# Block-sparse attention and a gated MLP on one core: leftover output products in other PSUM banks, two stores on another queue

## The chip, the cores and the metric

The kernel runs on one core of one Trainium2 chip. The metric is the device time of one execution in microseconds (us). Each engine of the core has its own instruction stream: PE (TensorE) multiplies matrices into PSUM, PEld is its weight load, ACT (ScalarE) and DVE (VectorE) read PSUM and write SBUF, POOL (GpSimd) does casts, SP (SyncE) mostly issues DMAs. Both SP and ACT can issue a DMA, and each instruction waits for semaphores of the work that it depends on.

## The reference

Attention under a block mask (window, first and last block, sampled blocks), and then a gated MLP with a spatial product per batch. B is 4, H 8, S 768, D 64, d_model 512, d_ff 1024. Cut to what matters:

```python
scores = np.where(mask, scale * q @ k.T, -1e9)
attn = exp(scores - max) ; attn = attn / (attn.sum(-1) + 1e-9)
x = (attn @ v).transpose(0, 2, 1, 3).reshape(B, S, H * D)
h = np.maximum(x @ w_in, 0.0)
u, v = h[..., :512], h[..., 512:]
v_n = (v - mean(v)) / sqrt(var(v) + 1e-6)
v_s = einsum('ts,bsd->btd', w_spatial, v_n) + b_spatial[None, :, None]
out = (u * v_s) @ w_out
```

## The kernel before, in words

The work is written out by hand, slot by slot (lines 880 to 898). In a slot PE makes the scores of one key chunk (`qk_full`, line 481) into a PSUM tile with tag "sc" (two buffers of two banks each), ACT takes the exponential, and seven slots later `av_full` (line 533) multiplies with the values into a tile with tag "av" (two buffers). DVE normalizes the result (`normalize`, lines 500 to 504: a reciprocal and a product). The MLP of batch b is a queue of single matmuls, `Moe` (line 627), dealt into the slots of batch b + 1; its PSUM tiles have the tags "moeA" and "moeB", one buffer each, in turn.

The MLP of a batch has six row chunks `tcc` of 128 tokens and four kinds of products, each a group of matmuls into one PSUM tile (`product`, line 608):

- v and u products (four matmuls), drained with a Relu by ACT or DVE.
- s products (six matmuls, the spatial product). DVE drains them into `un` (line 687), and SP then issues a DMA transpose of `un` into `gt` (line 697), two chunks at a time, or one at a time for the last two chunks of the last batch.
- o products (four matmuls with `gt` as weights), here called o0 to o5. ACT or DVE copies the tile to `osb` (six buffers, lines 714 and 715), and a DMA stores it (line 716). For batch 2, ACT copies o0, o2 and o4, and DVE o1, o3 and o5. For the last batch the even ones go to ACT, the odd to DVE, and o5 is made in two halves of 256 columns: the first is copied by DVE and stored by SP, the second copied and stored by ACT.

When the slots end, `last_x` (line 825) empties what is left of the queue, the **leftover**: three o products of batch 2, o3, o4 and o5. By then `ended` is set. It then begins the MLP of batch 3: the first matmuls of v0 and v1, six transposes of the last attention output into a bank of the "moe" pair, two DVE copies of that (`xt`), and the rest. From there no attention is left.

The PSUM tile of a product comes from `moe_ps` (line 598). While attention runs it is the "moe" pair. For the leftover and for all of batch 3, the deque `tail_tags` turns through "moe", "av" and "sc", so that all six buffers are used in turn. So in the kernel before, o3 has a tile of the "moe" pair (the one that o1 had), o4 one of "av", o5 one of "sc".

The stores of batch 3 in the kernel before: o0 by ACT; o1 to o4 and the first half of o5 by SP; the second half of o5 by ACT. SP issues the four transposes of batch 3 ahead of them, here T01, T23, T4 and T5 by their chunks; T45 is the last transpose of batch 2. DMAs of SP are the queue q1 of the profile, those of ACT q10.

Of the kernel before, what the change touches and what calls it, by code (L numbers as in the profile page):

```python
# [10 lines left out]
FP32 = mybir.dt.float32  # L11
# [15 lines left out]
def kernel(  # L27
# [16 lines left out]
    nc = tc.nc  # L44
# [27 lines left out]
    psum = ctx.enter_context(tc.tile_pool(name="psum", bufs=1, space=bass.MemoryType.PSUM))  # L72
# [219 lines left out]
    def moe_tag():  # L292
        moe_tags.rotate(1)
        if moe_tags[0] in held:
            moe_tags.rotate(1)
        return moe_tags[0]
# [301 lines left out]
    def moe_ps(last):  # L598
        if not (last or ended):
            return psum.tile([128, 512], FP32, tag=moe_tag(), bufs=1, name="ps_moe")  # L600
        tail_tags.rotate(1)
        if tail_tags[0] == "sc":
            return psum.tile([128, 1024], FP32, tag="sc", bufs=2, name="ps_sc")[:, 0:512]
        if tail_tags[0] == "moe":
            return psum.tile([128, 512], FP32, tag=moe_tag(), bufs=1, name="ps_t")
        return psum.tile([128, 512], FP32, tag="av", bufs=2, name="ps_t")

    def product(n, lhs, rhs, last, done, w=512):
        ref = {}
        out = []  # L610
        for i in range(n):
            def run(i=i):
                if i == 0:
                    ref["ps"] = moe_ps(last)
                nc.tensor.matmul(out=ref["ps"][:, 0:w], lhsT=lhs(i), rhs=rhs(i),  # L615
                                 start=(i == 0), stop=(i == n - 1))
                if i == n - 1:
                    done(ref["ps"][:, 0:w])
            out.append(run)
        return out  # L620
# [6 lines left out]
    class Moe:  # L627
# [75 lines left out]
        def o_product(self, tcc):  # L703
            steps = []
            osb = {}
            parts = 2 if self.last and tcc == NCH - 1 else 1
            w = DM // parts
            for i in range(parts):
                cs = slice(i * w, (i + 1) * w)

                def done(ps, i=i, cs=cs):
                    if i == 0:
                        osb["t"] = work.tile([128, DM], FP32, tag="osb", bufs=6, name="osb")
                    on_act = (tcc + i) % 2 == 0 if self.last else tcc in O_ACT[self.b]
                    (act_copy if on_act else dve_copy)(osb["t"][:, cs], ps)
                    (nc.scalar if i or (self.last and tcc == 0) else nc.sync).dma_start(
                        out=out[self.b].rearrange("(p c) d -> c p d", c=NCH)[tcc][:, cs],
                        in_=osb["t"][:, cs])
                steps += product(NDH, lambda d: self.gt[:, tcc, d, :],
                                 lambda d, cs=cs: w_out_t[:, d, cs], self.last, done, w)  # L720
            return steps
# [208 lines left out]
```

## Time and profile before

| what | us |
|---|---|
| time before, median of 3 runs | 209.9 (209.7 to 210.19) |
| the profiled execution's own time | 209.46 |
| its span, first to last instruction | 207.7 |
| PE busy | 201.7 (97%) |
| ACT busy | 166.9 (80%) |
| DVE busy | 128.9 (62%) |
| attention ends, leftover begins (PE) | about 177 |
| last matmul begins | 203.6 |

A line of the timeline has the start in us, the length, the engine, the line of the kernel, the operation, its tiles (out<-in) and shape, a count of merged instructions, and in brackets the idle time of the engine before it with what ended it. "SPq" and "ACTq" are the sequencers of these engines, which issue DMAs. The chain is the work that ended last, followed back from its end; its pieces have start, length, engine, tile and line. A DMA issue's last number is the time from issue to landing in us. The granted TensorE clock was 1.0 throughout.

### The profile page before, as it was taken

The numbers are of one execution on the slowest core, as the hardware profiler recorded it, in microseconds if no ns is written. First come the engines' busy times: TensorE is split into PE (matmuls) and PEld (weight loads), VectorE is DVE, ScalarE is ACT, GpSimd is POOL, SyncE is SP. The second block draws the span as 40 slices with busy tenths as digits, with TensorE's granted clock in tenths as the row PEclk, the third lists the DMA queues.
The fourth block names the chain that finished last, engine by engine and source line by source line (L and its number), as shares of the span: only waits on it lengthen the run. The fifth ranks groups of instructions, "written<-read, shape, count | busy, mean of one in ns | idle before, by whom it ended". The sixth has DMA issues, their size and how long they took to land.

```text
span 207.7 us, 5257 instructions
## 1 busy us (share of the span) xinstructions
PE 201.7 (97%) x2128; PEld 126.8 (61%) x2128; DVE 128.9 (62%) x287; ACT 166.9 (80%) x222; POOL 74.5 (36%) x117
## 2 busy tenths in 40 slices
PE   7899999999999999999999999999999999999992
PEld 6689778756666666665556555556555655444441
DVE  7688697789644454558797445448785345476541
ACT  5999999999999999889999878988999882276021
POOL 6999898585680421400726303100201000012000
PEclk9999999999999999999999999999999999999999
DMA  5999999999999999999948548994101063810475
GB/s 138 355 364 365 359 402 248 234 270 332 275 292 246 206 302 209 324 282 280 298 54 225 143 91 261 189 267 91 31 3 38 3 88 67 286 55 0 50 186 219
DMA packets 65579, 42.21 MB, mean 203 GB/s; under 512 B 46740, under 2 KB 60436, under 8 KB 65556
## 3 DMA queue, kind: packets, MB, share of 16 engines
q1 hardware_dynamic: 64980, 41.30, 77.3%
q10 hardware_dynamic: 576, 0.59, 0.9%
q8 instruction: 16, 0.26, 0.5%
q14 instruction: 7, 0.06, 0.1%
HBM read 24.38 MB, written 6.29 MB: 148 GB/s over the span
## 4 chain that ended last, share of the span: by engine, by line
PE 92%; ACT 5%; DVE 1%; issue 0%; ACTq 0%
PE ps_moe L615 32%; PE ps L487 23%; PE ps_av L538 13%; PE ps_t L615 9%; PE ps L474 6%; ACT a_all L479 4%; PE ps_sc L615 4%; PE ps_av L520 4%; PE wps L182 1%; PE ps L302 1%; PE ps_av L302 1%; DVE osb L221 0%; ACT kq L224 0%; PE mq L309 0%; ACT osb L224 0%
## 5 line engine op out<-in xcount | busy, mean ns | idle before, releaser
L491 ACT ACTIVATE a_all<-ps 128x768 bf16<-128x768 f32 x144 | 112.7, 811 | 11.9 <-PE ps L487 5.4
L487 PE MATMUL ps<-kq 88*128 88x384 bf16 x288 | 70.4, 325 | 0.0
L538 PEld LDWEIGHTS <-a_all 128*128 128x128 bf16 x864 | 45.2, 97 | 20.0
L538 PE MATMUL ps_av<-vv,a_all 128*128 128x65 bf16 x864 | 49.8, 193 | 0.0
L487 PEld LDWEIGHTS <-kq 88*128 88x128 bf16 x288 | 27.8, 97 | 29.2 <-issue 0.3
L615 PE MATMUL ps_moe<-w_in_t,xt 128*128 128x512 bf16 x144 | 43.2, 378 | 0.0
L479 ACT ACTIVATE a_all<-ps 128x1024 bf16<-128x1024 f32 x36 | 34.1, 1028 | 1.8 <-PE ps L474 1.5
L615 PE MATMUL ps_moe<-vn,w_spt 128*128 128x512 bf16 x108 | 33.5, 378 | 0.0
L654 POOL TENSOR_SCALAR std<-mv 128x3 f32<-128x3 f32 (+1 forms) x9 | 2.9, 318 | 71.7 <-DVE mv L651 57.1
L138 POOL CAST nat<-st_k 128x768 bf16<-128x768 f32 (+2 forms) x18 | 13.8, 770 | 31.3 <-DMA st_k<-in_k_dram 31.0
L502 DVE RECIPROCAL rc<-ps_av 128x6 f32<-128x6 f32 (+1 forms) x36 | 6.7, 187 | 26.5 <-PE ps_av L538 23.7
L687 DVE SCALAR_TENSOR_TENSOR un<-ps_moe,b_col,un 128x512 bf16<-128x512 f32 x18 | 13.5, 749 | 14.8 <-PE ps_moe L615 14.8
L474 PE MATMUL ps<-kq 88*128 88x256 bf16 (+3 forms) x140 | 21.6, 275 | 1.0 <-ACT a_all L479 0.5
L615 PEld LDWEIGHTS <-xt 128*128 128x128 bf16 x192 | 15.4, 98 | 7.5 <-DVE xt L221 0.2
L503 DVE TENSOR_TENSOR xn<-ps_av,rc 128x384 bf16<-128x384 f32 (+1 forms) x36 | 18.5, 513 | 1.2
L615 PE MATMUL ps_moe<-w_out_t,gt 128*128 128x512 bf16 x60 | 17.6, 378 | 0.0
L650 DVE BATCH_NORM_STATS2 stats<-vn 128x6 f32<-128x512 bf16 x24 | 16.4, 684 | 1.3 <-ACT vn L645 0.9
L474 PEld LDWEIGHTS <-kq 88*128 88x128 bf16 (+1 forms) x140 | 12.7, 97 | 5.4 <-DVE kq L221 1.0
L138 POOL CAST nat<-st_q 128x768 bf16<-128x768 f32 (+2 forms) x21 | 14.4, 688 | 2.7 <-DMA st_q<-in_q_dram 2.2
L188 DVE TENSOR_SCALAR vn<-ps_moe 128x512 bf16<-128x512 f32 x18 | 12.3, 686 | 4.6 <-PE ps_moe L615 4.5
L615 PEld LDWEIGHTS <-w_spt 128*128 128x128 bf16 x144 | 11.7, 98 | 5.2
L221 DVE COPY kq<-tt 64x1536 bf16<-64x1536 bf16 x24 | 13.9, 581 | 0.4
(85 smaller groups left out, 207.4 us busy)
## 6 DMA issues: line engine op xcount, KB each, us to landing
st_v<-in_v_dram SPq DMA_DIRECT2D x16, 384.0 KB, 5.6
st_k<-in_k_dram SPq DMA_DIRECT2D x15, 384.0 KB, 4.7
out_dram<-osb SPq DMA_DIRECT2D x22, 256.0 KB, 2.7
st_q<-in_q_dram SPq DMA_DIRECT2D x12, 384.0 KB, 4.6
w_f<-in_moe_w_in_dram SPq DMA_DIRECT2D x6, 256.0 KB, 6.7
ws_f<-in_moe_w_spatial_dram SPq DMA_DIRECT2D x4, 384.0 KB, 7.3
w_f<-in_moe_w_out_dram SPq DMA_DIRECT2D x4, 256.0 KB, 4.0
st_q<-in_q_dram SPq DMA_DIRECT2D x6, 128.0 KB, 5.3
```

The lines of the kernel that those rows point to most:

```text
L138: eng.tensor_copy(out=dst, in_=src)
L188: nc.vector.tensor_scalar(out=out, in0=in0, scalar1=s1, scalar2=s2, op0=o0, **kw)
L221: nc.vector.tensor_copy(out=o, in_=i)
L474: nc.tensor.matmul(out=ps[:, at:at + n * TW], lhsT=kq[0:kr, h, ci * 128:(ci + 1) * 128], rhs=kq[0:kr, h, qcols(t0, n)], start=True, stop=True)
L479: nc.scalar.activation(out=out, in_=ps, func=AF.Exp, scale=0.125)
L487: nc.tensor.matmul(out=ps[:, hf * 512:hf * 512 + HALF], lhsT=kq[0:KR, j % H, ci * 128:(ci + 1) * 128], rhs=kq[0:KR, j % H, S + hf * HALF:S ...
L491: nc.scalar.activation(out=a_ref["h", j][:, ci, :].rearrange("p (b c) -> p b c", b=2), in_=ps.rearrange("p (b c) -> p b c", b=2)[:, :, 0:H ...
L503: nc.vector.tensor_tensor(out=out, in0=ps[:, :, 0:D], in1=rc[:, 0:n].to_broadcast([128, n, D]), op=ALU.mult)
L538: nc.tensor.matmul(out=av_ref[j][:, qc, 0:VA], lhsT=a_ref["h", j][:, ci, qc * 128:(qc + 1) * 128], rhs=vv[p % NVV][:, h, ci, 0:VA], start= ...
L615: nc.tensor.matmul(out=ref["ps"][:, 0:w], lhsT=lhs(i), rhs=rhs(i), start=(i == 0), stop=(i == n - 1))
L650: nc.vector.bn_stats(out=stats, in_=self.vn[:, tcc, :])
L687: nc.vector.scalar_tensor_tensor(out=self.un[:, tcc, :], in0=ps, scalar=b_col[:, tcc:tcc + 1], in1=self.un[:, tcc, :], op0=ALU.add, op1=AL ...
```

## The change

Two edits. `moe_ps` gives the leftover products of batch 2 tiles with the tag "sc" alone, and leaves `tail_tags` unturned for them: o3 and o5 share one of the two buffers, o4 has the other. And the stores of o1 and o2 of the last batch are issued by ACT.

```diff
     def moe_ps(last):
         if not (last or ended):
             return psum.tile([128, 512], FP32, tag=moe_tag(), bufs=1, name="ps_moe")
+        if not last:
+            return psum.tile([128, 1024], FP32, tag="sc", bufs=2, name="ps_sc")[:, 0:512]
         tail_tags.rotate(1)
         if tail_tags[0] == "sc":
             return psum.tile([128, 1024], FP32, tag="sc", bufs=2, name="ps_sc")[:, 0:512]
...
                     (act_copy if on_act else dve_copy)(osb["t"][:, cs], ps)
-                    (nc.scalar if i or (self.last and tcc == 0) else nc.sync).dma_start(
+                    (nc.scalar if i or (self.last and tcc < 3) else nc.sync).dma_start(
                         out=out[self.b].rearrange("(p c) d -> c p d", c=NCH)[tcc][:, cs],
                         in_=osb["t"][:, cs])
```

In the built program no engine's instructions change order but for ACT and SP at the end. On PE the waits move: o3 waits for no copy any more, o5 waits for DVE (the copy of o3), v0 of batch 3 no longer waits for ACT, the six transposes wait for ACT (the copy of o2) in place of DVE, and u0 waits for ACT (the copy of o4). On ACT the order at the end becomes: copy o0, store o0, store o1 (waits for DVE's copy of o1), copy o2, store o2, copy o4, copy of the second half of o5, its store.

## The prediction

> **What bounds the kernel now.** I read the page's first and fourth parts, then the chain in order of time over the last 40 us, then the timeline in narrow windows where the chain leaves PE, and last the DMA views. The page says that PE is the engine, and the chain agrees.
>
> ```profile
> PE 201.7 (97%) x2128; PEld 126.8 (61%) x2128; DVE 128.9 (62%) x287; ACT 166.9 (80%) x222; POOL 74.5 (36%) x117
> PE 92%; ACT 5%; DVE 1%; issue 0%; ACTq 0%
> ```
>
> So a change elsewhere counts only where PE stands still. The chain in order of time shows where it does at the end of the attention, and at the end of the kernel:
>
> ```profile
> 175.70 0.20 PE ps_av L538 x6
> ...
> 175.92 0.21 DVE rc L502
> ...
> 176.15 0.24 DVE xn L503
> ...
> 176.62 0.69 DVE osb L221
> ...
> 177.36 1.89 PE ps_t L615 x8
> 179.24 0.86 PE ps_sc L615 x4
> ...
> 200.30 0.91 PE ps_sc L615 x4
> ...
> 203.46 0.45 PE ps_t L615 x4
> ...
> 203.98 0.38 ACT osb L224
> ```
>
> Between 175.90 and 177.36 the chain (rows of bare issue time are left out) runs through DVE: the reciprocal and product of the last attention tile, and behind them in DVE's order the copy of o1 (osb, 176.62 to 177.31). o3 has the tile of the "moe" pair that o1 had, so PE waits for that copy. In narrow windows, PE around that wait:
>
> ```profile
> 176.80 0.38 PE L615 MATMUL ps_moe<-w_out_t,gt 128*128 128x512 bf16 x1
> 177.36 0.38 PE L615 MATMUL ps_t<-w_out_t,gt 128*128 128x512 bf16 x1 [0.18 <-DVE osb L221]
> ```
>
> The idle time in the bracket (0.18) counts from the modelled end of the matmul before. Starts are the better measure: four matmuls of 512 columns take 0.86 in the chain, so they start 0.216 apart. After 176.80 the next could start at 177.02. It starts at 177.36: PE loses **0.34 us** here.
>
> **The change part by part. First edit: o3, o4 and o5 in the score tiles.** No matmul is added or removed. o3's wait goes: both score buffers were last read by the exponentials of the attention, and the last of these ended at 171.81:
>
> ```profile
> 168.17 3.64 ACT L491 ACTIVATE a_all<-ps 128x768 bf16<-128x768 f32 x4 [0.35 <-PE ps L487]
> ```
>
> So o3 can start at 177.02, 0.34 earlier. What is late next? Two things: the weights of o4, and o5's tile.
>
> The weights of o4 are the `gt` of chunks 4 and 5, by T45 on SP's queue. The timeline of SP, the DMA view of that one issue, and PEld's timeline:
>
> ```profile
> 174.92 1.23 SPq L697 DMA_TRANSPOSE gt<-un  x1
> gt<-un SPq DMA_TRANSPOSE x1, 3.0
> 178.01 0.30 PEld L615 LDWEIGHTS <-gt 128*128 128x128 bf16 x2
> ```
>
> T45 lands at 174.92 + 3.0 = 177.92, give or take 0.05 of rounding. A weight load starts along with the matmul before its own: in the kernel before, o4's first load is the one at 178.01, beside o3's last matmul (177.36 + 3 x 0.216 = 178.01), and o4 starts at 178.22. So T45 came just in time. With o3 at 177.02, that load would be due at 177.66 and o4 at 177.88. It has to wait for T45 until about 178.0. How a matmul follows such a late load is seen at o2 of the last batch, whose weights also came late:
>
> ```profile
> 200.17 0.11 PEld L615 LDWEIGHTS <-gt 128*128 128x128 bf16 x2 [0.36 <-DMA gt<-un]
> 200.17 0.39 PE L615 MATMUL ps_sc<-w_out_t,gt 128*128 128x512 bf16 x1
> ```
>
> The matmul starts with its load, and the product takes 0.91 in the chain where others take 0.86, 0.04 of it the wait itself. So I put o4 at the load's 178.01 and 0.02 for the late load: 178.03, against 178.22 before. Of the 0.34 us, **0.19 us** is left. The bounds: if T45 lands earlier in an execution, o4 is at 177.88 and all 0.34 stays; if it lands later than here, o4 waits for it in both kernels and nothing is gained. The transposes of `un` landed after 2.5 to 3.8 us in the last 58 us:
>
> ```profile
> DMA to landing us min/median/max: 2.5/3.2/3.8
> ```
>
> I keep 3.0, since T45 is issued at the same moment in both kernels with the same queue ahead of it.
>
> o5 now waits for DVE's copy of o3, in the same buffer. Before:
>
> ```profile
> 178.42 0.69 DVE L221 COPY osb<-ps_t 128x512 f32<-128x512 f32 x1 [1.11 <-PE ps_t L615]
> 179.28 0.60 ACT L224 ACTIVATE osb<-ps_t 128x512 f32<-128x512 f32 x1 [1.47 <-PE ps_t L615]
> ```
>
> That copy starts 178.42 - 177.36 = 1.06 after its product's first matmul, and takes 0.69. With o3 at 177.02 it runs from 178.08 to 178.77, and DVE is free by then (o1's copy ends at 177.31). PE follows a copy after 0.05 (177.31 to 177.36), so o5's tile is free at 178.82. PE arrives at 178.03 + 0.86 = 178.89. Covered by 0.07, and what hides it is the wait for T45: with T45 early, PE would arrive at 178.74 and wait 0.08, so the best case is 0.34 - 0.08 = 0.26. Behind o5 on PE stand v0, v1 and the transposes, which would all move with it. Their own new waits are old by then: the transposes wait for the copy of o2, which ACT begins at 177.21 and ends at 177.81, and start near 181; u0 waits for the copy of o4, which ends at 179.88 before, over 1.5 us ahead of u0 at 181.57.
>
> ```profile
> 177.21 0.60 ACT L224 ACTIVATE osb<-ps_moe 128x512 f32<-128x512 f32 x1 [1.50 <-PE ps_moe L615]
> 181.57 0.38 PE L615 MATMUL ps_sc<-w_in_t,xt 128*128 128x512 bf16 x1
> ```
>
> From there to the end the chain is PE almost without a break, and the transposes of the last batch hang on PE's own products, so 0.19 us early there is 0.19 us early at the end.
>
> **Second edit: the stores of o1 and o2 by ACT.** The timeline of the end:
>
> ```profile
> 199.51 1.22 SPq L697 DMA_TRANSPOSE gt<-un  x1
> 200.15 0.35 ACTq L716 DMA_DIRECT2D out_dram<-osb  x1
> 200.34 0.69 DVE L221 COPY osb<-ps_t 128x512 f32<-128x512 f32 x1 [0.91 <-PE ps_t L615]
> 201.06 0.42 SPq L716 DMA_DIRECT2D out_dram<-osb  x1
> 201.25 0.60 ACT L224 ACTIVATE osb<-ps_sc 128x512 f32<-128x512 f32 x1 [1.13 <-PE ps_sc L615]
> 201.87 0.33 SPq L716 DMA_DIRECT2D out_dram<-osb  x1
> 202.13 0.81 PE L615 MATMUL ps_t<-w_out_t,gt 128*128 128x512 bf16 x3
> 202.84 0.22 PEld L615 LDWEIGHTS <-gt 128*128 128x128 bf16 x3 [0.41 <-DMA gt<-un]
> 202.85 0.39 PE L615 MATMUL ps_sc<-w_out_t,gt 128*128 128x256 bf16 x2
> 202.97 0.60 ACT L224 ACTIVATE osb<-ps_t 128x512 f32<-128x512 f32 x1 [1.13 <-PE ps_t L615]
> 204.40 0.35 ACTq L716 DMA_DIRECT2D out_dram<-osb  x1
> out_dram<-osb ACTq DMA_DIRECT2D x1, 128.0 KB, 2.0
> ```
>
> SP loses two issues and ACT gains two of 0.35. The first waits for DVE's copy of o1, which ends at 201.03; the copy of o2 is queued behind it. The issue then runs to 201.41, and that copy starts near 201.45 instead of 201.25, 0.2 late, ends at 202.05, and the second issue ends at 202.42. The next work of ACT, the copy of o4, starts at 202.97: 0.5 us of slack hides both. Nobody waits for the copy of o2 but its store, since o5's two halves have other buffers. What sets the end is PE's last matmul, ACT's copy of the last half, its store at 204.40 and 2.0 us to landing, 206.40; none of these is touched. The SP stores that remain are issued when their copies end, so SP was no bottleneck either: **0 us**, between -0.25 and +0.6 by the rivals below.
>
> **The sum.** 209.46 - 0.19 = 209.27 for the profiled execution, whose span would go from 207.7 to 207.5. The median of the runs shown is 0.44 above that execution, so for a median I take 209.9 - 0.19 = **209.7 us**, 0.09% faster. About 0.2%, 0.42 us, is what a measurement of this kernel can tell from no change.
>
> **The rivals.**
>
> *Landing first.* T45 lands sooner and o5's tile becomes the bound: gain 0.26, 209.6 us. For it speaks the 2.5 us that the shortest transpose took, against it that T45 moves two chunks, and the shortest one chunk.
>
> *No gain.* The change doesn't do what it says: T45 lands later than here, and PE waits for it instead of for the copy, in both kernels alike. 209.9 us. For it speaks that 3.0 is below the median 3.2; against it that DVE's copy, not the DMA, ended the wait here.
>
> *Slower: the last transpose shares the DMA engines with one more store.* o5 waits for T5, issued at 199.51 and not there before 202.8 (the 202.84 load above): 3.3 us. T4, as large, had none of ACT's packets beside it:
>
> ```profile
> 198.19 1.23 SPq L697 DMA_TRANSPOSE gt<-un  x1
> gt<-un SPq DMA_TRANSPOSE x1, 2.5
> ```
>
> T5 does have some, from ACT's store of o0. The DMA packets from 201.6 to 202.0, where T5's closing writes fall, by queue:
>
> ```profile
> q10 hardware_dynamic: 75, 0.14, 96.3%
> q1 hardware_dynamic: 12, 0.00, 4.0%
> ```
>
> So a store on ACT's queue goes along with 0.8 us more for T5. If ACT's store of o1 does as much again, T5 lands 0.8 us later, PE already stands there (o4's last three matmuls start from 202.13 on, so o5 is due at 202.78 and starts at 202.85), and the end moves by 0.8 - 0.19: 210.5 us. It decides from a delay of 0.19 on. Against it: the packets of ACT's first store begin some 1.1 us after its issue (200.15, and at 201.6 they fill the engines), so those of o1's store would begin near 202.1, when T5's are almost through. The Trainium skill, "DMA: Bandwidth & Descriptors", under "Queues, rings and completion order", has each DMA engine take packets in turn from the queue rows that have work, and under "Issuing engines are not separate DMA queues" that another issuing engine saves only issue time. By that rule the second edit can win nothing in transfer, and a store that stood behind T5 in SP's row stands beside it in ACT's. The two rows above agree with the sharing; what it costs T5 here no row shows.
>
> *More than the sum.* The DMA engines are over 90% busy in the last stores, and with two stores out of SP's queue the last ones land up to 0.25 us earlier: 209.9 - 0.19 - 0.25 = 209.5 us. Against it: the last store takes 2.0 us, as short as any, so nothing seems to stand before it.
>
> **How the numbers follow.** Forecast (209.7) 0.55; landing first (209.6) 0.13; no gain (209.9) 0.12; slower (210.5) 0.10; more than the sum (209.5) 0.10. Runs of one kernel lie between 209.7 and 210.19, so each case has some 0.25 us around it. Faster by over 0.2%: most of the last case and a tail of the first two, 0.17. Slower by over 0.2%: the slow case and a little of no gain, 0.10. Within 0.2%: 0.73. The range: from the best case of the first edit, 209.9 - 0.34, less 0.25, 209.3, to no gain and 0.3 above, 210.2; the rest of the slow case and of the best one is left out.
>
> **What would show it.** PE's first leftover matmul would start 0.22 after the one before it and not 0.56; o4's first load would stand some 0.3 us behind that, put down to the DMA of `gt`; o5 would wait for no copy; the copy of o2 at the end would start 0.2 us later against PE than now, with the copy of o4 unmoved. Wrong would be: o5 of batch 2 waiting for DVE, a wait of PE ahead of o5 of the last batch well above the 0.07 of now, or a last store that takes other than 2.0 us.

## The result, and the profile after

The changed kernel takes 209.25 us in the median (208.96 to 209.64, 12 runs), the kernel before 209.91 (209.59 to 210.31, 12 runs). The ratio is 0.9969, with a 95% interval of 0.996 to 0.9978: **faster by 0.66 us, 0.31%**. The forecast was 0.19 us faster, 209.7, and a range from 209.3; the time lies just under the range, and the gain is over three times the forecast. All medians and ratios here are of fast runs: one run of e2 (300.36 us), one of e6 (351.59) and two of the kernel before (425.54 and 1192.2) were in a slower state and are left out.

The profiled execution of the changed kernel hides this: 209.45 us, where that of before had 209.46. Its page, first the span, then parts 1 and 4:

```profile
span 207.6 us, 5255 instructions
PE 202.7 (98%) x2128; PEld 127.2 (61%) x2128; DVE 129.9 (63%) x287; ACT 167.0 (80%) x222; POOL 75.4 (36%) x117
PE 93%; ACT 5%; issue 0%; DVE 0%; ACTq 0%
```

So two executions must first be laid on each other. The exponentials of the first phase (line 479), all 36, with the start of the first and the last one behind the durations, before and then after:

```profile
L479 ACT ACTIVATE a_all<-ps x36: 1018/1023/1065, 5.6 to 39.8; 128x1024 bf16<-128x1024 f32 x36
```

```profile
L479 ACT ACTIVATE a_all<-ps x36: 1017/1024/1055, 6.1 to 40.5; 128x1024 bf16<-128x1024 f32 x36
```

The first exponential starts 0.5 us later and the last one 0.7 us. The two chains show one source of it, the first four score matmuls, before:

```profile
4.93 0.61 PE ps L474 x4
```

and after:

```profile
5.04 1.03 PE ps L474 x4
```

Nothing that the diff touches has run by then, and from 24 us on the two run in step, 0.67 us apart, until the leftover. It is the luck of one execution: the kernel before alone spreads over 0.7 us. What the change does must be read from the start of o2's last matmul on (176.80 before, 177.47 after), and the time of an execution from several of them.

The chain of the changed kernel from there, in order of time, beside the one in the prediction:

```profile
176.56 1.29 PE ps_moe L617 x6
177.85 2.73 PE ps_sc L617 x12
180.58 1.29 PE ps_t L617 x6
...
200.77 0.86 PE ps_sc L617 x4
201.63 1.73 PE ps_t L617 x8
203.36 0.56 PE ps_sc L617 x4
203.92 0.45 PE ps_t L617 x4
...
204.44 0.38 ACT osb L224
```

DVE is gone from it. The twelve leftover matmuls take 2.73, where 12 x 0.216 is 2.59: 0.14 us of waiting is inside. The timeline of PE, PEld and DVE there, then T45's issue in SP's timeline, and its time to landing in the DMA view:

```profile
177.25 0.59 PE L617 MATMUL ps_moe<-w_out_t,gt 128*128 128x512 bf16 x2
177.69 0.38 PE L617 MATMUL ps_sc<-w_out_t,gt 128*128 128x512 bf16 x1
178.67 0.11 PEld L617 LDWEIGHTS <-gt 128*128 128x128 bf16 x2 [0.46 <-DMA gt<-un]
178.75 0.69 DVE L221 COPY osb<-ps_sc 128x512 f32<-128x512 f32 x1 [0.77 <-PE ps_sc L617]
179.12 0.81 PE L617 MATMUL ps_sc<-w_out_t,gt 128*128 128x512 bf16 x3
```

```profile
175.59 1.23 SPq L699 DMA_TRANSPOSE gt<-un  x1
```

```profile
gt<-un SPq DMA_TRANSPOSE x1, 3.0
```

o2's last matmul starts at 177.47 (the second of the first row) and o3 at 177.69, 0.22 later instead of 0.56. o4's weights wait for T45, which lands at 178.6, and are loaded at 178.67. o5 (the last of the three in the last row) starts at 179.55, 2.08 after o2's last matmul; before it was 2.28. PE is 0.20 us earlier, and at the start of ACT's last copy 0.21 (26.97 behind o2's last matmul instead of 27.18): in this trace the first edit did as the prediction had it.

The other 0.43 us lie behind the last store. The end of SP's stream before, from the last wait for a store's landing (L925 is the end of the program):

```profile
L925 SPq EVENT_SEMAPHORE  x1: 28/28/28, 206.4 to 206.4; - x1
L925 SPq DRAIN  x1: 7/7/7, 206.5 to 206.5; - x1
L925 SPq DRAIN  x1: 130/130/130, 206.8 to 206.8; - x1
```

and after:

```profile
L927 SPq EVENT_SEMAPHORE  x1: 28/28/28, 206.8 to 206.8; - x1
L927 SPq DRAIN  x3: 7/7/7, 206.9 to 207.2; - x3
```

Behind them all engines wait for each other (each has its last waits at 207.1 and 207.6). Between SP's first and second DRAIN stand 0.35 us in the kernel before, and the second one takes 130 ns instead of 7. In the changed kernel all three take 7 ns, and the second starts 0.05 behind the first. From the landing of the last store to the end of the span it is 207.67 - 206.40 = 1.27 us before and 207.64 - 206.80 = 0.84 after. Nothing is computed or moved in that time.

Counted from the start of the span, SP has 211 instructions before and 207 after: each store that ACT took over is a DMA and a wait fewer. The second DRAIN before is instruction 207 (the first being 0); the changed kernel has none of that number. And instruction 79, 128 places ahead of it, also has an idle time ahead of it that no semaphore explains, here with the wait just before it, in the view of line 444 (the start stands behind the durations in ns):

```profile
L444 SPq EVENT_SEMAPHORE  x1: 17/17/17, 65.3 to 65.3; - x1
L444 SPq DMA_TRANSPOSE tt<-nat x1: 2801/2801/2801, 65.7 to 65.7; - x1
```

0.455 us pass between the wait's end and the transpose, the same 0.455 in the changed kernel. The page's third part has two queues that bring instructions: q8 in 16 packets of 16 KB, q14 in 7 packets of 0.06 MB together, some 8 KB each:

```profile
q8 instruction: 16, 0.26, 0.5%
q14 instruction: 7, 0.06, 0.1%
```

The Trainium skill, "Runtime: NRT & Kernel Launch", under "Instruction fetch mechanics", has each engine's instructions come in blocks by a queue of its own, 256 at a time, with the crossing mostly hidden; "Perfetto Trace Analysis", under "The 4-stage abstract model", gives an instruction 64 bytes; an estimate from that figure is 256 instructions in a packet of q8 and 128 in one of q14. That instructions come in blocks on queues apart from the data's agrees with q8 and q14, but with seven packets where SP passes two such places, q14 is not SP's alone. The distance of 128 and the idle 0.35 to 0.46 us do not agree with 256 and mostly hidden, and the measurement decides.

When these packets come can be read too. The DMA view of the kernel before for 206.4 to 207.6 us has no packet of any queue, and in the one for 207.6 to 208.2 stands the next packet of q14, at 207.76:

```profile
q14 instruction: 1, 0.01, 3.2%
```

So SP did not stand still until a packet had landed: the packet comes behind the place. In all 14 traces a packet of q14 starts 0.2 to 0.8 us after the end of instruction 79, and in the seven that have an instruction 207, 0.5 to 1.1 us after the end of that one; none of either queue lies in the idle time ahead of them. In the seven whose SP stream ends before 207, the last packet starts 1.0 us after the end of the span.

### The profile page after: what moved, and what is told of

Its sections match the earlier page's. It is cut to its first block, busy times and chain, and to the rows that moved or that the text cites. A ratio compares the mean times of both kernels' runs of the same rounds, so it can differ in the third digit from the quotient of the medians.

```text
span 207.6 us, 5255 instructions
## 1 busy us (share of the span) xinstructions
PE 202.7 (98%) x2128; PEld 127.2 (61%) x2128; DVE 129.9 (63%) x287; ACT 167.0 (80%) x222; POOL 75.4 (36%) x117
## 4 chain that ended last, share of the span: by engine, by line
PE 93%; ACT 5%; issue 0%; DVE 0%; ACTq 0%
PE ps_moe L617 32%; PE ps L487 23%; PE ps_av L538 13%; PE ps_t L617 8%; PE ps L474 6%; PE ps_sc L617 5%; ACT a_all L479 5%; PE ps_av L520 4%; PE wps L182 1%; PE ps L302 1%; PE ps_av L302 1%; PE mq L309 0%; ACT osb L224 0%; PE psq L317 0%; PE ps L317 0%
## 5 line engine op out<-in xcount | busy, mean ns | idle before, releaser
L138 POOL CAST nat<-st_k 128x768 bf16<-128x768 f32 (+2 forms) x18 | 14.6, 810 | 30.8 <-DMA st_k<-in_k_dram 29.9
L221 DVE COPY kq<-tt 64x1536 bf16<-64x1536 bf16 x24 | 14.4, 598 | 0.4
```

The costliest lines, as they stand in the source:

```text
L138: eng.tensor_copy(out=dst, in_=src)
L221: nc.vector.tensor_copy(out=o, in_=i)
```

## The experiments

The theory after the result: two gains that have nothing to do with each other, 0.21 us at the leftover (bounded by T45) and 0.43 at SP's exit, set by *where* in SP's stream the exit stands and not by which stores moved. Rival 1: moving the last stores helps by itself, by less load on SP's queue at the end. Rival 2: the first edit does all of it.

**e1_leftover_only** has the first edit alone:

```diff
+        if not last:
+            return psum.tile([128, 1024], FP32, tag="sc", bufs=2, name="ps_sc")[:, 0:512]
```

> The first edit alone: the leftover products in the score tiles, the stores as before. Theory (two separate gains: 0.21 us at the leftover, bounded by the transpose T45, and some 0.4 us at SP's exit, where SP's stream of instructions is 4 shorter and no longer has its 207th, ahead of which it stood 0.35 us): 209.7 us, 0.2 under before; SP's exit as slow as before, a DRAIN of 130 ns at the end, and 1.27 us from the landing of the last store to the end of the span. Rival 1 (the second edit's stores are what helps, by less load on SP's queue in the last 6 us): also 209.7. Rival 2 (the first edit does it all, and the gain behind it was hidden in the profiled execution): 209.25 us.

Measured: 209.84 against 209.94, ratio 1.0003 (0.9993 to 1.0012). In the trace the last copy of ACT is 0.22 us earlier, from o2's last matmul on, and the exit takes 1.27 us as before, with the DRAIN of 130 ns. The trace bears out the theory; the times do not, since 0.21 us would be a ratio of 0.9990, which lies outside the interval. So the kernel was run again below. Rival 2 falls.

**e2_stores_only** has the second edit alone:

```diff
-                    (nc.scalar if i or (self.last and tcc == 0) else nc.sync).dma_start(
+                    (nc.scalar if i or (self.last and tcc < 3) else nc.sync).dma_start(
```

> The second edit alone: the stores of o1 and o2 of the last batch by ACT, the leftover as before. Theory (instruction count of SP): 209.5 us, 0.43 under before; PE loses its 0.56 between the starts of o2's last and o3's first matmul as before; from the landing of the last store to the end of the span 0.84 us and not 1.27. Rival 1 (fewer stores in SP's queue): 209.5 as well, but by earlier landings of the last stores. Rival 2 (first edit alone): 209.9, as before.

Measured: 209.34 against 209.94, ratio 0.9977 (0.9966 to 0.9988). PE's path is unchanged (0.01 us), the last store takes 1.97 us to land, as before (2.00), and the exit 0.85 instead of 1.27. So the second edit carries most of the gain, and no more than 0.03 us of it is in the stores.

**e3_before_plus4** adds four instructions to SP in the kernel before:

```diff
-        when({4: 13, 5: 22, 6: 31}.get(p, g - 34), c(load, p, "k"), c(load, p, "q"), c(load, p, "v"))
+        when({4: 13, 5: 22, 6: 31}.get(p, g - 34), c(load, p, "k"), c(load, p, "q"),
+             *([c(load, p, "v", H0), c(load, p, "v", H1)] if p in (12, 13, 14, 15) else [c(load, p, "v")]))
```

> The kernel before with 4 instructions MORE on SP and nothing else: the loads of v for the last four head pairs are issued in two halves each, long before the end. Theory (place in SP's instruction stream): SP's 207th instruction is then one of the waits for the last stores, and the 0.35 us pass while SP waits anyway: 209.5 us, 0.4 under before although SP has more to do; last landing to end of span about 0.85 us. Rival 1 (load on SP's queue): 209.9, or a little more. Rival 2: 209.9.

Measured: 210.21, ratio 1.0021 (1.0001 to 1.0041). A miss. The DMAs take eight semaphores in turn, so with four DMAs more the last store had the semaphore that SP waits for *first*; instruction 207, now the third of the waits at the end, came after the landing and not before it. Its idle time is there (0.367 us, where the waits beside it follow in 0.04 to 0.06), but nothing hides it, and the exit takes 1.48 us. What it tells is that the idle time went to another kind of instruction with the number 207.

**e4_after_plus4** has the same four instructions more in the changed kernel.

> The changed kernel with the same 4 instructions more on SP: its stream ends at the same place as before's. Theory: the 0.4 us at the exit come back, 209.65 us, a DRAIN of 130 ns at the end, 1.27 us from the last landing to the end. Rival 1 (the last stores): 209.25, since the stores at the end are those of the changed kernel. Rival 2: 209.25.

Measured: 210.04, ratio 1.0009 (0.9999 to 1.0019), so the whole gain is gone although both edits stand. The end of its SP stream:

```profile
L928 SPq DRAIN  x1: 7/7/7, 207.1 to 207.1; - x1
L928 SPq DRAIN  x1: 130/130/130, 207.5 to 207.5; - x1
```

The same two DRAINs, the same 0.35 us, the same 130 ns: its second DRAIN is instruction 207 again. The exit takes 1.56 us and not 1.27, since the last store's semaphore came first here too, and the other four waits stand behind it. Rival 1 falls with this run: the stores at the end are those of the changed kernel.

**e5_midstores_act** moves other stores, of batch 2, in the kernel before:

```diff
-                    (nc.scalar if i or (self.last and tcc == 0) else nc.sync).dma_start(
+                    (nc.scalar if i or (self.last and tcc == 0) or (self.b == 2 and tcc in (0, 2, 4)) else nc.sync).dma_start(
```

> The kernel before, with three stores of BATCH 2 (o0, o2 and o4, some 25 us before the end) issued by ACT instead of SP, at a time when ACT is idle; the stores of the last batch and the leftover as before. SP's stream is shorter by some five instructions, and the DMAs keep their order. Theory (place in SP's instruction stream): no 0.35 us ahead of SP's 207th instruction, 0.85 us from the last landing to the end of the span, 209.45 us, 0.45 under before. Rival (the queue of the last stores matters): 209.9, since these are untouched.

Measured: 210.24 against 209.86, ratio 1.0019 (1.001 to 1.0027): slower. The exit is the short one, 0.84 us. But T45 is late. The timeline with T45's issue, the store of o0 on ACT and the load of o4's weights, and T45's time to landing in the DMA view:

```profile
175.36 1.23 SPq L697 DMA_TRANSPOSE gt<-un  x1
176.19 0.35 ACTq L716 DMA_DIRECT2D out_dram<-osb  x1
179.47 0.55 PEld L615 LDWEIGHTS <-gt 128*128 128x128 bf16 x4 [1.15 <-DMA gt<-un]
```

```profile
gt<-un SPq DMA_TRANSPOSE x1, 4.1
```

4.1 us instead of 3.0: the store of o0, on SP's queue behind T45 before, now runs beside it on ACT's, and o4 starts 0.82 us later. This is the mechanism of the prediction's slower rival, at another place and with about its price. 0.82 lost and 0.43 won make 0.39, and 0.38 was measured.

**e9_midstores_late** is the same without o0's store, and with o5's in its place, which is issued when T45 has long landed:

```diff
+                    (nc.scalar if i or (self.last and tcc == 0) or (self.b == 2 and tcc in (2, 4, 5)) else nc.sync).dma_start(
```

> The kernel before, with the stores of o2, o4 and o5 of batch 2 by ACT and the store of o0 left on SP; the last batch as before. (With o0's store on ACT, T45 landed 2.19 us after the start of o2's last matmul instead of 1.17, and o4 waited for it.) Theory: T45 lands at 1.17 and o4 starts at 1.42 as before, SP's stream ends ahead of its 207th instruction, 0.85 us from the last landing to the end of the span: 209.5 us, 0.4 under before, with the last stores untouched. Rival (the queue of the last stores matters): 209.9.

Measured: 209.42 against 209.93, ratio 0.9976 (0.9963 to 0.9989). The second edit's gain (0.9977), with every store of the last batch where it was before, and the leftover as before. Its DRAINs follow each other:

```profile
L925 SPq DRAIN  x1: 13/13/13, 206.7 to 206.7; - x1
L925 SPq DRAIN  x1: 7/7/7, 206.8 to 206.8; - x1
```

**e8_before_plus8** adds eight instructions to SP, so that the semaphores keep their order:

```diff
+        when({4: 13, 5: 22, 6: 31}.get(p, g - 34), *[c(load, p, nm, hs) for nm in "kqv"
+               for hs in ((H0, H1) if p >= 12 and nm != "q" else (BOTH,))])
```

> The kernel before with 8 instructions MORE on SP, and every semaphore of the last stores as before: the loads of k and of v for the last four head pairs are issued in two halves each. (With four more, the last store's semaphore was the first that SP waited for at the end, and the place fell behind it.) Theory: SP's 207th instruction is now the wait ahead of the last SP store; the 0.35 us delay that store, which lands about when ACT's does, and the exit is free of them: 0.95 us from the last landing to the end or less, 209.6 us, 0.3 under before although SP has more to do. Rival (what counts is how many instructions or DMAs SP has): 209.9 or more.

Measured: 210.08, ratio 1.0009 (1.0 to 1.0018). Half a miss. The exit takes 0.85 us as said. But instruction 207 is the wait ahead of SP's last store (0.355 us idle before it), and that store then runs beside ACT's last one: they land after 2.3 and 2.6 us where both had taken 2.0.

```profile
out_dram<-osb SPq DMA_DIRECT2D x1, 128.0 KB, 2.3
out_dram<-osb ACTq DMA_DIRECT2D x1, 128.0 KB, 2.6
```

0.43 us less at the exit, 0.61 more to the last landing. The cost moved with the place; it wasn't hidden there. The packet of q14 moved with it: it starts at 205.44, 1.1 us behind the wait, in the DMA view for 205.4 to 205.8:

```profile
q14 instruction: 1, 0.01, 4.8%
```

**e10_before_plus16** is the same for the last eight head pairs (`p >= 8`).

> The kernel before with 16 instructions MORE on SP: the loads of k and v of the last eight head pairs in two halves each; the semaphores of the last DMAs as before. (With eight more, the 0.35 us fell ahead of SP's last store and came back there.) Theory: SP's 207th instruction is now a wait that stands right behind T5's issue, where SP waits about 0.26 us for DVE's copy of o1 anyway; nothing after it is late, 0.85 us from the last landing to the end: 209.5 us, 0.4 under before with 16 DMAs more on SP. Rival (the number of DMAs or instructions on SP): 210 or more.

Measured: 210.4 with a wide spread (209.07 to 211.56), ratio 1.0015 (0.9992 to 1.0039): inconclusive as a time. The profiled execution falls 0.6 us further behind that of the kernel before between 88 and 95 us, where PE stands idle for 0.44 us until a transpose lands (at 92.41); that the halved loads held this transpose up is likely, but not shown. The exit takes 0.84 us; instruction 207 is a wait near 202 with 0.346 idle before it. Instruction 79 is a load here, and has its idle time as the transpose had: 63.36 + 1.07 is 64.43, and the next starts 0.45 later.

```profile
63.36 1.07 SPq L110 DMA_DIRECT2D st_k<-in_k_dram  x2
64.88 0.38 SPq L110 DMA_DIRECT2D st_q<-in_q_dram  x1
```

**e6_t45_split** tests the bound at the leftover: in the changed kernel T45 is issued as two transposes, and T01 and T23 of batch 1 as one, so that SP's count stays.

```diff
+                if self.b == 1 and tcc == 1:
+                    return
-                if self.last and tcc >= NCH - 2:
+                if self.b >= 2 and tcc >= NCH - 2:
                     g0 = tcc
+                elif self.b == 1 and tcc == 3:
+                    g0 = 0
```

> The changed kernel, with T45 of batch 2 issued as two transposes of one chunk each, and the two transposes T01 and T23 of batch 1 as one of four chunks, so that SP has as many instructions as in the changed kernel. Theory (T45 bounds o4): from the start of o2's last matmul, o3 at 0.22 as in the changed kernel, o4 at 1.08 instead of 1.21, and o5 then waits for DVE's copy of o3, at 2.03 instead of 2.08; the last matmul 0.05 earlier than in the changed kernel. Time 209.2. Rival (something else holds o4, as PE's own order): o4 stays at 1.21.

Measured: 209.29, ratio 0.9961 (0.9946 to 0.9976). After o2's last matmul o4 starts at 1.08 and o5 at 2.03, as expected to the hundredth. With T45 out of the way o5 waits for the copy of o3.

**e7_o5_in_av** gives o5 a tile of its own on top of that:

```diff
         if not last:
+            ended.append(True)
+            if len(ended) == 4:
+                return psum.tile([128, 512], FP32, tag="av", bufs=2, name="ps_t")
             return psum.tile([128, 1024], FP32, tag="sc", bufs=2, name="ps_sc")[:, 0:512]
```

> As the run before this, and o5 of batch 2 in a tile of the attention's output (tag av) instead of sharing o3's tile. Theory: o5 has no copy to wait for any more, o4 at 1.08, o5 at 1.94, v0 at 2.81 after the start of o2's last matmul, so all of the 0.34 us is kept, 0.13 more than in the changed kernel: 209.1 us. Rival (o5 was not held by the copy): o5 as in the run before.

Measured: 209.09 against 209.86, ratio 0.9962 (0.995 to 0.9974). o4 at 1.08, o5 at 1.94, v0 at 2.81: the leftover's matmuls stand in one row.

```profile
176.10 1.30 PE ps_moe L620 x6
177.40 1.73 PE ps_sc L620 x8
179.12 2.16 PE ps_t L620 x10
```

1.73 for eight, with no wait in it. In the trace this is 0.13 us better than the changed kernel; the times can't tell the two apart.

**e11_leftover_again** and **e12_changed_again** are the first edit alone and the changed kernel once more, on one chip.

> The first edit alone once more, beside the changed kernel on the same chip: the first time the trace showed 0.22 us between the start of o2's last matmul and the end, but the times only 0.1 (209.84 against 209.95). Theory: 209.7, 0.2 under before, 0.43 above the changed kernel. Rival: the gain of the first edit is lost somewhere that the trace does not show, 209.9.

> The changed kernel once more, on the same chip as the run before this. Theory: 209.25 us, and 0.43 under the first edit alone.

Measured: 209.68, ratio 0.9989 (0.9979 to 0.9999), and 209.12, ratio 0.9965 (0.9951 to 0.9979). This time the first edit alone gives 0.25 us; with e1's 0.10 the trace's 0.21 lies between. The difference of the two kernels, 0.56, is nearer to 0.43 than to nothing.

The path from the start of o2's last matmul to the end of the span, from each trace, against the medians. The first three columns of times are pieces of that path: to the issue of ACT's last store, from there to the last landing, from there to the end; the sum is told against before's 30.87.

| kernel | to last issue | to landing | to the end | sum, against before | median, against before |
|---|---|---|---|---|---|
| before | 27.60 | 2.00 | 1.27 | 0 | 0 |
| changed | 27.39 | 1.95 | 0.84 | -0.70 | -0.66 |
| e12 the same again | 27.39 | 1.99 | 0.84 | -0.65 | -0.81 |
| e1 leftover only | 27.38 | 1.99 | 1.27 | -0.23 | -0.10 |
| e11 the same again | 27.37 | 2.04 | 1.28 | -0.18 | -0.25 |
| e2 stores only | 27.59 | 1.97 | 0.85 | -0.46 | -0.60 |
| e9 other stores | 27.58 | 2.01 | 0.86 | -0.42 | -0.51 |
| e5 with o0's store | 28.42 | 1.95 | 0.84 | +0.33 | +0.38 |
| e3 before, 4 more on SP | 27.51 | 2.09 | 1.48 | +0.21 | +0.27 |
| e4 changed, 4 more on SP | 27.38 | 2.09 | 1.56 | +0.15 | +0.10 |
| e8 before, 8 more on SP | 27.58 | 2.61 | 0.85 | +0.17 | +0.22 |
| e10 before, 16 more on SP | 27.68 | 2.06 | 0.84 | -0.30 | +0.47 |
| e6 T45 split | 27.34 | 1.99 | 0.86 | -0.68 | -0.57 |
| e7 T45 split, o5 apart | 27.25 | 1.95 | 0.84 | -0.83 | -0.77 |

But for e10, which loses its time ahead of this path, the sums follow the medians within 0.16 us over a range of 1.2.

## Why the prediction was wrong, point by point

- **First edit, right in mechanism and, in the traces, in size.** 0.34 us of stall gone, T45 late next: forecast 0.19, and 0.20 at o5 and 0.21 at the last copy in the trace. The times alone are less sure (1.0003 in e1, 0.9989 in e11); the changed kernel (0.9969 and 0.9965) lies some 0.2 us under the second edit's gain alone (0.9977 in e2, 0.9976 in e9). o5's tile was free in time, and the next bound when T45 was taken away, as the working had it (e6: o5 at 2.03, from 2.08).
- **Second edit: the step that failed.** "What sets the end is PE's last matmul, ACT's copy of the last half, its store at 204.40 and 2.0 us to landing, 206.40; none of these is touched." True up to the landing (2.00 us before, 1.97 in e2), but the sum stopped there, and took the 1.27 us from the landing to the end of the span for a constant. 0.43 us of it were SP's, and the edit took four instructions out of SP's stream. The text counted "SP loses two issues" as queue time, and did not ask what the end of the program waits for. The row that would have asked is the 130 ns DRAIN of the end, beside two of 7 ns, on the engine that leaves last.
- **The rival "more than the sum"** came nearest in time (209.5), with a little over half of the 0.43 and the wrong reason: the last store took 1.95 us to land, where it had taken 2.00.
- **The rival "slower"** did not come about: T5 landed 3.3 us after its issue as before (o5's load at 203.31, T5 issued at 199.98), as the prediction's argument against this rival had it (that ACT's second store came too late to stand beside T5 was not tried by itself). Its mechanism is real, though: in e5 a store on ACT's queue beside T45 cost it 1.0 us.

```profile
199.98 1.22 SPq L699 DMA_TRANSPOSE gt<-un  x1
200.62 1.26 ACTq L718 DMA_DIRECT2D out_dram<-osb  x2
201.93 0.60 ACT L224 ACTIVATE osb<-ps_sc 128x512 f32<-128x512 f32 x1 [1.34 <-PE ps_sc L617]
203.31 0.77 PEld L617 LDWEIGHTS <-gt 128*128 128x128 bf16 x8 [0.45 <-DMA gt<-un]
203.40 0.60 ACT L224 ACTIVATE osb<-ps_t 128x512 f32<-128x512 f32 x1 [0.87 <-PE ps_t L617]
```

- **ACT's order** went as said: the two issues end the copy's wait 0.2 us late (201.93, which is 0.21 later against PE), and the copy of o4 is where it was against PE.

What is shown is that the idle time of 0.35 us stands ahead of SP's instruction 207, whatever that instruction is (a DRAIN before, in e1, e4 and e11, a wait in e3, e8 and e10), and that the exit is short in every kernel whose SP stream ends before it or has passed it. That the place is a boundary between blocks of instructions is argued from the distance of 128, the size of q14's packets and the packet that follows the place wherever it is moved. What SP does in the 0.35 us stays open: it doesn't wait for a packet that is still on its way, since none lies in that time.

## What to carry to other kernels

Read the end of the program too: from the last landing to the end of the span, engine by engine, and ask of the one that leaves last what it did there, since a change that moves instructions from one engine to another moves its exit. Differences of a few tenths of a microsecond are read from a common point in two traces, not from two spans, when the start alone varies by more than that. And when a wait is removed, working out the next two arrivals (here a transpose and a copy) gave the gain in the trace to 0.02 us.

## What the runs showed of the hardware

- SP stood still for 0.35 to 0.46 us at places 128 instructions apart in its stream (79 and 207, counted from the start of the span), with DMA, wait and DRAIN instructions alike. It costs where nothing hides it: 0.43 us at the exit (with the DRAIN's 130 ns), and in e8, ahead of SP's last store, 0.61 us to the last landing, as that store then ran beside ACT's. A packet of instructions on q14 starts 0.2 to 1.1 us after the end of each of these instructions, and none lies in the idle time.
- The waits for stores at the end stand in a fixed order of eight semaphores. With the last store on the first of them, the others follow its landing one by one, and the exit is longer by 0.2 to 0.3 us (1.48 in e3 and 1.56 in e4, instead of 1.27).
- A 256 KB store on ACT's queue beside a transpose on SP's queue made the transpose land after 4.1 us instead of 3.0, where the same store stood behind it on SP's queue (before and e9).
